# Folding later batches at the end of the first layer, with the shared tokens' unfolded queries in a stationary tile of their own

## The chip, the cores and the metric

One core of one Trainium2 chip runs the whole program. The metric is device time in microseconds (us), the median of several executions; lower is better. PE is TensorE (matmuls; PEld its weight loads), DVE is VectorE, ACT is ScalarE, POOL is GpSimd, SP issues most of the DMAs.

## The reference

Eight batches, eight heads, 576 tokens, 64 dimensions for each head, all in float32.

```python
q_s = softmax(q, over the 64 dimensions);  k_s = softmax(k, over the 576 tokens)
x   = q_s @ (k_s^T @ v)                      # per batch and head, then heads side by side: 576 x 512
u   = x + real(fft(fft(x, over tokens), over the 512 columns))
un  = (u - mean(u)) / sqrt(var(u) + 1e-6)    # over the 512 columns
out = u + relu(un @ w_ch1) @ w_ch2           # 512 -> 2048 -> 512
```

## The kernel before

**Tokens.** Of the 576 tokens of a batch, 512 lie in four "own" tiles of 128 rows, x(c, u) with c and u in 0 and 1. The other 64 are "shared" tokens: those of two batches fill one tile of 128 rows, and the four such tiles of all batches make a ninth group of the same size as a batch. The two layers run over groups in the order: batches 0 to 6, the shared group, batch 7.

**Attention** (`attention`, L430) is a list of steps for keys (four pairs of heads), shared queries (every other batch, for two batches at once) and own queries. The keys' softmax times v goes into `kvr`, a tile of four 128x128 blocks, one for a pair of heads. Own queries are exponentiated (L599), transposed on PE (L623), copied by ACT (L630), multiplied by `kvr` (L658) and copied by ACT to x (L665). For shared queries, `t_turn` (L633) transposes and copies both batches' 64 tokens into the columns 64 to 127 of `F`, and `t_fold` (L638) makes sums and differences of mirrored tokens, which the Fourier transform needs, into the columns 0 to 63 (17, 16, 16 and 15 of them, packed). So `F` holds, for each of four pairs of heads and each of two batches, one stationary tile of 128 columns: 64 folded, 64 unfolded. `t_times_kv` (L667), the last step of attention, multiplies them by `kvr` in four matmuls (L673): rows 0 to 63 of the result are the folded tokens, rows 64 to 127 are this batch's shared tokens. ACT copies the result to `g` (L676), and its lower half to the shared tile xs (L677). DVE then folds the columns of `g` (L678, L680, L681).

**Transform** (`transform`, L686). For batches after the first it is a list: four fold steps, one step that does nothing (batches 2 to 7), five blocks. The folds are `tokens_folded` (L699: sums on POOL, differences on DVE, of the own tiles), `columns_folded` (L705), `by_frequency` (L714) and `folded`, which makes the last DVE folds (L720, L721) and starts the next batch's first two key loads, each with a tiny DVE instruction (`gate`, L495) that ties the keys' use to the fold. The blocks are matmuls with the cosine and sine tables `ft` (L752 with the folded own tokens, L755 with `g`). Then follow the transform over columns (`mix_own`, `mix_shared`), which adds to x, and `norm` (statistics, normalization, transposes and the sums of its quarters, L369 to L372).

**Layers.** From the second group on, both layers (`up`, L945, and `down`, L982) use seven half-size products in place of eight (`strassen`, L906), in the order 1, 6, 5, 7, 2, 4, 3, over three PSUM banks `ba`, `bb` and `bc`. The first layer is four jobs of seven products, each product eight matmul instructions of 256 columns; the second layer is one job of seven products of 32 such instructions. (A float32 matmul in the code is two instructions in the profile.) Products 6, 7 and 4 add up in `bb`: after 6, DVE reads the bank into `u2` (L925), after 7 into `u3` (L929), and 7 and 4 are then added to the bank by matmuls without a start. In the first layer DVE adds the results (L968), ACT applies relu (L964, L969), and POOL makes the sums that the second layer's products need (`a_side`, L362 to L365). In the second layer POOL adds intermediate values to x (L1007).

**Order.** The main function (L1054) mixes lists: `one` is the attention of the next batch, `two` the transform, mixes and, behind them, `norm` of the next group. `merged(flat(jobs), one)` spreads `one` evenly over the first layer's steps, `merged(down, two + ...)` spreads the others over the second layer's. The program is then built by a framework that keeps each engine's queue in an order of its own planning, with priorities that follow this order, so that neighbouring steps may change places. Each engine then takes its queue in order. The first group (batch 0 in the layers, batch 1 in attention and transform) has hand-written gaps in place of `merged`.

Of the kernel before, what the change touches and what calls it, by code (L numbers as in the profile page):

```python
# [40 lines left out]
F32 = mybir.dt.float32  # L41
I32, U32 = mybir.dt.int32, mybir.dt.uint32
ACT = mybir.ActivationFunctionType
ALU = mybir.AluOpType
AX = mybir.AxisListType

P = 128
B, H, S, DH = 8, 8, 576, 64
D = H * DH
FF = 4 * D  # L50
NR = H // 2
# [5 lines left out]
MO = S // 4  # L57
ME = MO + 1
Q = 32
W = 2 * Q  # L60
NT = Q // 2 + 1
# [22 lines left out]
def mixed(main, side):  # L84

    steps = []
    for i, step in enumerate(main):
        steps.append(step)
        steps += side[i * len(side) // len(main):(i + 1) * len(side) // len(main)]
    return steps  # L90


def merged(main, side):
    for step in mixed(main, side):
        step()
# [28 lines left out]
class _Block:  # L124
    def __init__(self, ctx, tc, q, kT, v, w1, w2, ft, cd, out):
        self.nc, self.tc = tc.nc, tc
        self.q, self.kT, self.v, self.w1, self.w2, self.out = q, kT, v, w1, w2, out
        self.ft_dram, self.cd_dram = ft, cd
        nc = self.nc
        pool = lambda name, **kw: ctx.enter_context(tc.tile_pool(name=name, bufs=1, **kw))  # L130
        self.const, self.work, self.small = pool("const"), pool("work"), pool("small")
        self.ps = pool("ps", space=bass.MemoryType.PSUM)
        self.dram = pool("dram", space=bass.MemoryType.DRAM)
        c = self.const
        self.ident = c.tile([P, P], F32, name="ident")
        make_identity(nc, self.ident[:])
        self.eps = c.tile([P, 1], F32, name="eps")
        nc.gpsimd.memset(self.eps[:], LN_EPS)
        self.kvr = []
        for b in range(2):  # L140
            t = c.tile([P, NR, P], F32, name=f"kvr{b}")
            nc.gpsimd.memset(t[:], 0.0)
            self.kvr.append(t)

        self.sn = []
        for i in range(2):
            t = c.tile([P, NN], F32, name=f"sn{i}")
            nc.gpsimd.memset(t[:], 0.0)
            self.sn.append(t)

        self.ZT = c.tile([P, KT, P], F32, name="ZT")

        self.Zr, self.ZTr = c.tile([P, HD], F32, name="Zr"), c.tile([P, P], F32, name="ZTr")
        self.kss = [c.tile([P, NC, P], F32, name=f"ks{i}") for i in range(2)]
        for t in (self.Zr, self.ZTr):
            nc.gpsimd.memset(t[:], 0.0)
        for t in self.kss:
            nc.gpsimd.memset(t[0:64, 4, :], 0.0)

        self.T, self.F = c.tile([P, 2 * NR, 4, NT], F32, name="T"), c.tile([P, 2 * NR, P], F32, name="F")  # L160
        nc.gpsimd.memset(self.T[:], 0.0)

        self.sign = c.tile([P, 1], F32, name="sign")
        nc.gpsimd.memset(self.sign[:], -1.0)
        nc.gpsimd.memset(self.sign[0:Q + 1], 1.0)
        d = self.dram
        self.w1s = [d.tile([P, 7, HD], F32, tag=f"w1s{p}", name=f"w1s{p}", bufs=1) for p in range(NP)]
        self.w2s = d.tile([7, P, NP, HD], F32, tag="w2s", name="w2s", bufs=1)

        self.big = c.tile([P, 3 * NF * D], F32, name="big")  # L170
        part = lambda i: self.big[:, i * NF * D:(i + 1) * NF * D].rearrange("p (f n) -> p f n", n=D)
        self.w1sb, self.w2sb, self.h0 = part(0), part(1), part(2)
        self.ft = c.tile([P, 4 * NM], F32, name="ft")
        self.cd = c.tile([P, 5 * QD + 1], F32, name="cd")
        self.xs, self.live, self.stream = {}, {}, {}
        self.turns = 0
        self.unused = None

        self.later = []

        self.words = [self.work.tile([P, 2, D], F32, tag=n, name="words", bufs=k) for n, k in (("xs", 2), ("x", 4), ("x", 4))]
# [122 lines left out]
    def tables(self):  # L304
        self.nc.sync.dma_start(self.ft[:], self.ft_dram)
        self.nc.sync.dma_start(self.cd[:], self.cd_dram)
# [326 lines left out]
    def t_turn(self, it):  # L633
        pt = self.turned_q(it)
        self.live.pop(it)
        self.nc.scalar.copy(self.F[:, :, W:], pt[:].rearrange("p r (e t) -> p (r e) t", t=W))

    def t_fold(self, it):  # L638

        V, G, T, F = self.nc.vector, self.nc.gpsimd, self.T, self.F  # L640
        q = F[:, :, W:]
        V.tensor_copy(T[:, :, 0:2, 0], q[:, :, 0:Q + 1:Q])
        for e, op, i in ((G, ALU.add, 0), (V, ALU.subtract, 2)):
            e.tensor_tensor(out=T[:, :, i, 1:NT], in0=q[:, :, 1:NT], in1=q[:, :, W - 1:W - NT:-1], op=op)
            e.tensor_tensor(out=T[:, :, 1 + i, 1:NT - 1], in0=q[:, :, Q - 1:Q - NT + 1:-1],
                            in1=q[:, :, Q + 1:Q + NT - 1], op=op)
        n = NT - 1
        pair = lambda a, step: F[:, :, a:a + 2 * step].rearrange("p r (k t) -> p r k t", t=step)[:, :, :, 0:n]
        V.tensor_tensor(out=pair(NT, NT + n - 2), in0=T[:, :, 0:3:2, 0:n], in1=T[:, :, 1:4:2, 0:n], op=ALU.subtract)
        G.tensor_tensor(out=pair(1, Q), in0=T[:, :, 0:3:2, 1:NT], in1=T[:, :, 1:4:2, 1:NT], op=ALU.add)  # L650
        V.tensor_tensor(out=F[:, :, 0:1], in0=T[:, :, 0, 0:1], in1=T[:, :, 1, 0:1], op=ALU.add)

    def q_times_kv(self, it):
        nc, (_, b, c, u) = self.nc, it
# [12 lines left out]
    def t_times_kv(self, b):  # L667
        nc, V = self.nc, self.nc.vector
        j, kvr = b % 2, self.kvr[b % 2]
        part = slice(W * j, W * j + W)  # L670
        px = self.acc((P, D))
        for r in range(NR):
            nc.tensor.matmul(px[:, r * P:(r + 1) * P], lhsT=self.F[:, 2 * r + j], rhs=kvr[:, r, :], start=True,  # L673
                             stop=True)
        g = self.halves()
        nc.scalar.copy(g[:, 0:D], px)  # L676
        nc.scalar.copy(self.xshared(b // 2)[part], px[W:])  # L677
        V.scalar_tensor_tensor(out=g[:, 1:HD], in0=g[:, D - 1:HD:-1], scalar=self.sign[:, 0:1], in1=g[:, 1:HD],  # L678
                               op0=ALU.mult, op1=ALU.add)
        V.tensor_tensor(out=g[:, NN:NN + QD], in0=g[:, 0:QD], in1=g[:, HD:QD:-1], op=ALU.subtract)  # L680
        V.tensor_tensor(out=g[:, 0:QD], in0=g[:, 0:QD], in1=g[:, HD:QD:-1], op=ALU.add)  # L681
        self.live["g", b] = g
# [371 lines left out]
def kernel(ctx: ExitStack, tc: tile.TileContext, q, kT, v, w1, w2, ft,  # L1054
# [27 lines left out]
    def norm(g):  # L1082
        def make():
            nexts[g], steps = blk.norm(g)
            return steps
        return late(make, 7)

    def flat(steps):
        return [s for step in steps for s in step]
# [17 lines left out]
    one, two = front(0)  # L1107
# [5 lines left out]
    for order, g in enumerate(groups):  # L1113
        loads = [] if g == 0 else None
        one, two = front(order + 1, loads) if order + 1 < B else (blk.later, [])
        if g == 0:
# [6 lines left out]
            n = 2 * NF - 10  # L1123
# [6 lines left out]
            turn = (0, 16, 19, 21, 23, 25)  # L1130
# [13 lines left out]
            at = 0  # L1144
# [15 lines left out]

        jobs, down = blk.up(order, nexts.pop(g)), blk.down(g, order)

        merged(flat(jobs), one)
        merged(down, two + (norm(groups[order + 1]) if order < B else []))


def tables():

    turn = lambda a, b, n: 2.0 * np.pi * (np.outer(a, b) % n) / n
    odd = np.concatenate([np.arange(129, 160, 2), np.arange(1, 128, 2), np.arange(287, 160, -2)])  # L1170
    even = np.concatenate([[0], np.arange(130, 159, 2), [288], np.arange(2, 129, 2), np.arange(286, 159, -2)])
    ft = np.zeros((P, 4 * NM), np.float32)
    a = turn(1 + np.arange(P), np.concatenate([odd, even]), S)
    ft[:, :NM], ft[:, NM:2 * NM] = np.cos(a), np.sin(a)
    row = P + np.arange(NT)
    row[0] = n = 0

    for i, (f, m, at, rows) in enumerate(((np.cos, even, MO, row), (np.cos, odd, 0, row[:-1]), (np.sin, odd, 0, row[1:]),
                                          (np.sin, even, MO, row[1:-1]))):
        at += (2 + i // 2) * NM  # L1180
        ft[n:n + len(rows), at:at + len(m)] = f(turn(rows, m, S))
        n += len(rows)
    d, n = np.arange(P), np.arange(QD)
    cd = np.zeros((P, 5 * QD + 1), np.float32)
    cd[:, :QD] = np.cos(turn(d, 2 * n + 1, D))
    cd[:, QD:NN] = np.cos(turn(d, 2 * np.arange(QD + 1), D))
    cd[:QD - 1, NN:NN + QD - 1] = np.sin(turn(d[1:], 2 * n[1:], D))
    cd[:, NN + QD - 1:D] = np.sin(turn(d + 1, 2 * n + 1, D))
    cd[:, D:] = 1.0 - 2.0 * (np.arange(QD + 1) % 2)
    return ft, cd  # L1190
# [28 lines left out]
```

## Time and profile before

| what | value |
|---|---|
| median of 3 runs (lowest to highest) | 1128.05 us (1124.97 to 1131.2) |
| profiled execution, its own time | 1128.05 us |
| its span, first to last instruction | 1126.2 us |
| mean granted PE clock | 0.991 |
| DMA, mean over the span | 172 GB/s |
| one period (a group's two layers) in the middle, 322.6 to 442.7 us | 120.1 us |

The busy share of an engine is an average over the span; the table of stretches in the next section gives it for single stages. The head, about 88 us, is batch 0's attention, transform and norm, with the weights' loads under way; then come batch 0's two plain layers until 199 us; then eight groups of two layers with seven products each.

### The profile page before, as it was taken

To read this page: it belongs to the slowest core of one execution; us is meant where nothing else is said; L and a number is where in the kernel's file an instruction comes from. 1 tells how busy PE (TensorE), PEld (TensorE's weight loads), DVE (VectorE), ACT (ScalarE), POOL (GpSimd) and SP (SyncE) were. 2 spreads that over 40 slices of the span, in tenths; PEclk is the share of its full clock that TensorE was granted. 3 is DMA by queue.
4 is the path that set the end of the run, shared out by engine and by line. 5 is a ranking of instruction groups with operands and counts; after the bars stand their busy time and mean duration, and the time that the engine had idled before them with its cause. 6 is when DMAs were issued, how large, how long until landed. Compare 5 with 4: busy or idle time off the path is not lost.

```text
span 1126.2 us, 14461 instructions
## 1 busy us (share of the span) xinstructions
PE 1088.4 (97%) x5376; PEld 909.9 (81%) x5376; DVE 545.4 (48%) x1121; ACT 403.5 (36%) x973; POOL 331.9 (29%) x303
## 2 busy tenths in 40 slices
PE   5789989999999999999999999999999999999997
PEld 4644545887888888898889888888889888888886
DVE  6694796368423734375344643583444352103301
ACT  6695434255233513362325332542334152201200
POOL 1065571235013510324024402251034203402320
PEclk8899999999999999999999999999999999999999
DMA  9555786464246534554356435642453444434451
GB/s 305 176 190 188 259 291 220 145 224 166 98 150 211 195 127 145 195 172 171 125 173 221 150 106 190 198 185 108 147 191 150 144 144 144 187 141 157 152 187 56
DMA packets 92581, 193.79 MB, mean 172 GB/s; under 512 B 23120, under 2 KB 59728, under 8 KB 85344
## 3 DMA queue, kind: packets, MB, share of 16 engines
q1 hardware_dynamic: 90712, 191.82, 49.9%
q10 hardware_dynamic: 1800, 1.05, 0.3%
q8 instruction: 43, 0.70, 0.2%
q14 instruction: 26, 0.21, 0.1%
HBM read 168.72 MB, written 28.31 MB: 175 GB/s over the span
## 4 chain that ended last, share of the span: by engine, by line
PE 81%; POOL 3%; issue 2%; ACT 1%; DVE 1%; ACTq 0%; POOLq 0%
PE bb L957 14%; PE bb L995 14%; PE bc L995 10%; PE ba L957 9%; PE bc L957 9%; PE ba L995 9%; PE acc L568 2%; PE acc L658 2%; PE bc L896 2%; PE acc L752 1%; PE acc L776 1%; PE acc L755 1%; PE tr L857 1%; PE tr L554 1%; PE tr L623 1%
## 5 line engine op out<-in xcount | busy, mean ns | idle before, releaser
L957 PE MATMUL bb<-unT,big 128*128 128x256 f32 x768 | 187.4, 381 | 0.2 <-DVE u L925 0.2
L995 PE MATMUL bb<-big 128*128 128x256 f32 x768 | 172.1, 379 | 0.0
L957 PEld LDWEIGHTS bb<-unT,big 128*128 128x128 f32 x768 | 142.8, 190 | 23.9 <-DVE u L925 3.0
L995 PEld LDWEIGHTS bb<-big 128*128 128x128 f32 x768 | 145.4, 190 | 20.3
L362 POOL TENSOR_TENSOR big<-big 128x512 f32<-128x512 f32 (+1 forms) x38 | 46.2, 1216 | 307.6 <-ACT big L969 306.8
L969 ACT ACTIVATE big<-big 128x512 f32<-128x512 f32 x96 | 60.3, 629 | 182.7 <-DVE big L968 182.2
L957 PE MATMUL bc<-unT,big 128*128 128x256 f32 x512 | 125.4, 379 | 0.0
L957 PE MATMUL ba<-unT,big 128*128 128x256 f32 x512 | 123.6, 379 | 0.2 <-ACT unT L861 0.2
L995 PE MATMUL bc<-big 128*128 128x256 f32 x512 | 116.0, 379 | 0.5 <-DVE x L1012 0.5
L995 PE MATMUL ba<-big 128*128 128x256 f32 x512 | 114.8, 379 | 0.0
L929 DVE TENSOR_TENSOR u<-bb,s 128x512 f32<-128x512 f32 x40 | 27.6, 691 | 173.1 <-PE bb L995 116.1
L995 PEld LDWEIGHTS bc<-big 128*128 128x128 f32 x512 | 96.1, 190 | 14.3 <-DVE x L1012 0.9
L995 PEld LDWEIGHTS ba<-big 128*128 128x128 f32 x512 | 95.7, 190 | 12.1
L957 PEld LDWEIGHTS bc<-unT,big 128*128 128x128 f32 x512 | 95.1, 190 | 12.6
L957 PEld LDWEIGHTS ba<-unT,big 128*128 128x128 f32 x512 | 95.1, 190 | 12.2 <-ACT unT L861 0.5
L370 POOL TENSOR_TENSOR unT<-unT 128x512 f32<-128x512 f32 x8 | 14.2, 1772 | 179.8 <-DVE unT L369 179.8
L607 ACT ACTIVATE q<-q,qm 128x64 f32<-128x64 f32 x240 | 61.6, 338 | 6.8 <-DVE qm L605 6.6
L925 DVE TENSOR_TENSOR u<-bb,s 128x512 f32<-128x512 f32 x40 | 27.5, 688 | 71.7 <-PE bb L957 38.7
L968 DVE TENSOR_TENSOR big<-bc,u 128x512 f32<-128x512 f32 x64 | 44.1, 689 | 22.8 <-PE bc L957 21.7
L1007 POOL TENSOR_TENSOR x<-x,u 128x512 f32<-128x512 f32 x14 | 17.7, 1267 | 118.8 <-DVE u L929 99.0
L861 ACT COPY unT<-tr 128x512 f32<-128x512 f32 x36 | 20.7, 585 | 79.9 <-PE tr L857 79.3
L968 DVE TENSOR_TENSOR big<-bb,s 128x512 f32<-128x512 f32 x32 | 22.1, 691 | 56.1 <-PE bb L957 56.1
(254 smaller groups left out, 1640.8 us busy)
## 6 DMA issues: line engine op xcount, KB each, us to landing
big<-w1s SPq DMA_DIRECT2D x64, 896.0 KB
big<-w2s SPq DMA_DIRECT2D x56, 1024.0 KB
big<-in_w_dram SPq DMA_DIRECT2D x21, 512.0 KB
q<-in_q_dram SPq DMA_DIRECT2D x27, 256.0 KB
k<-in_kT_dram SPq DMA_DIRECT2D x24, 288.0 KB
v<-in_v_dram SPq DMA_DIRECT2D x24, 256.0 KB
words<-in_w_dram SPq DMA_DIRECT2D x8, 512.0 KB
mirror<-x SPq DMA_DIRECT2D x14, 256.0 KB
```

Source lines behind the costliest of these rows:

```text
L362: e1.tensor_tensor(out=to(4), in0=at(2), in1=at(3), op=ALU.add)
L568: nc.tensor.matmul(pk, lhsT=ks[:, c, :], rhs=v[:, c, :], start=(c == 0), stop=(c == NC - 1))
L607: nc.scalar.activation(heads[:, h, :], heads[:, h, :], ACT.Exp, bias=m[:, h:h + 1])
L658: nc.tensor.matmul(px[:, r * P:(r + 1) * P], lhsT=qT[:, r, :], rhs=self.kvr[b % 2][:, r, :], start=True, stop=True)
L861: nc.scalar.copy(unT[:, u:u + 3:2, :, cols], pt[:].rearrange("p (a k) t -> p a k t", a=2))
L896: nc.tensor.matmul(po[:], lhsT=h[:, f, i * P:(i + 1) * P], rhs=self.w2sb[:, f, :], start=(f == 0), stop=(f == NF - 1))
L925: V.tensor_tensor(out=temp("u2"), in0=box["bb"][:], in1=box["s1"][:], op=ALU.add)
L929: V.tensor_tensor(out=temp("u3"), in0=box["bb"][:], in1=box["s1"][:], op=ALU.add)
L957: nc.tensor.matmul(bank()[:, i, :], lhsT=w[:, WA_AT[m], k * P:(k + 1) * P], rhs=unT[:, B_AT[m], k, :], start=first and i == 0 and k == 0, ...
L968: V.tensor_tensor(out=hp(i), in0=bank[:], in1=u[:], op=ALU.add)
L969: nc.scalar.activation(hp(i), hp(i), ACT.Relu)
L995: nc.tensor.matmul(bank()[:, i, :], lhsT=h[p][:, A_AT[m], i * P:(i + 1) * P], rhs=w[:, p, :], start=first and i == 0 and p == 0, stop=p == ...
```

## The change

`F` is laid out anew: for each pair of heads and batch, four blocks of 32 columns, 17 of them used, and nothing unfolded; it is zeroed at the start. The unfolded transposed queries of both batches go to a new tile `tq`, from which `t_fold` reads. `t_times_kv` multiplies `F` by `kvr` in four matmuls as before, and then, in a new group of four into another PSUM buffer, `tq` by `kvr`; ACT copies the 64 rows that belong to this batch to xs. The last fold instructions of `t_fold` are one on each of POOL and DVE in place of one on POOL and two on DVE. Signs and tables follow the new layout. In the main loop, for the groups after the first, the first four steps of `two`, the folds, are put behind attention in `one`, so that they are spread over the end of the first layer and not over the start of the second; this concerns batches 2 to 7.

```diff
-        self.T, self.F = c.tile([P, 2 * NR, 4, NT], F32, name="T"), c.tile([P, 2 * NR, P], F32, name="F")
-        nc.gpsimd.memset(self.T[:], 0.0)
+        self.T, self.F = c.tile([P, 2 * NR, 4, NT], F32, name="T"), c.tile([P, 2 * NR, 4, Q], F32, name="F")
+        for t in (self.T, self.F):
+            nc.gpsimd.memset(t[:], 0.0)
...
-        nc.gpsimd.memset(self.sign[:], -1.0)
-        nc.gpsimd.memset(self.sign[0:Q + 1], 1.0)
+        nc.gpsimd.memset(self.sign[0:W], 1.0)
+        nc.gpsimd.memset(self.sign[W:], -1.0)
...
     def t_turn(self, it):
         pt = self.turned_q(it)
         self.live.pop(it)
-        self.nc.scalar.copy(self.F[:, :, W:], pt[:].rearrange("p r (e t) -> p (r e) t", t=W))
+        self.tq = self.work.tile([P, NR, P], F32, tag="tq", name="tq", bufs=1)
+        self.nc.scalar.copy(self.tq[:], pt[:])
 
     def t_fold(self, it):
 
         V, G, T, F = self.nc.vector, self.nc.gpsimd, self.T, self.F
-        q = F[:, :, W:]
-        V.tensor_copy(T[:, :, 0:2, 0], q[:, :, 0:Q + 1:Q])
-        for e, op, i in ((G, ALU.add, 0), (V, ALU.subtract, 2)):
+        q = self.tq[:].rearrange("p r (e t) -> p (r e) t", t=W)
+        V.tensor_copy(T[:, :, 0:3:2, 0], q[:, :, 0:Q + 1:Q])
+        for e, op, i in ((G, ALU.add, 0), (V, ALU.subtract, 1)):
             e.tensor_tensor(out=T[:, :, i, 1:NT], in0=q[:, :, 1:NT], in1=q[:, :, W - 1:W - NT:-1], op=op)
-            e.tensor_tensor(out=T[:, :, 1 + i, 1:NT - 1], in0=q[:, :, Q - 1:Q - NT + 1:-1],
+            e.tensor_tensor(out=T[:, :, 2 + i, 1:NT - 1], in0=q[:, :, Q - 1:Q - NT + 1:-1],
                             in1=q[:, :, Q + 1:Q + NT - 1], op=op)
-        n = NT - 1
-        pair = lambda a, step: F[:, :, a:a + 2 * step].rearrange("p r (k t) -> p r k t", t=step)[:, :, :, 0:n]
-        V.tensor_tensor(out=pair(NT, NT + n - 2), in0=T[:, :, 0:3:2, 0:n], in1=T[:, :, 1:4:2, 0:n], op=ALU.subtract)
-        G.tensor_tensor(out=pair(1, Q), in0=T[:, :, 0:3:2, 1:NT], in1=T[:, :, 1:4:2, 1:NT], op=ALU.add)
-        V.tensor_tensor(out=F[:, :, 0:1], in0=T[:, :, 0, 0:1], in1=T[:, :, 1, 0:1], op=ALU.add)
+        for e, op, i in ((G, ALU.add, 0), (V, ALU.subtract, 1)):
+            e.tensor_tensor(out=F[:, :, i::2, 0:NT], in0=T[:, :, 0:2], in1=T[:, :, 2:4], op=op)
...
         g = self.halves()
         nc.scalar.copy(g[:, 0:D], px)
-        nc.scalar.copy(self.xshared(b // 2)[part], px[W:])
+        px = self.acc((P, D))
+        for r in range(NR):
+            nc.tensor.matmul(px[:, r * P:(r + 1) * P], lhsT=self.tq[:, r, :], rhs=kvr[:, r, :], start=True, stop=True)
+        nc.scalar.copy(self.xshared(b // 2)[part], px[part])
...
         jobs, down = blk.up(order, nexts.pop(g)), blk.down(g, order)
 
+        if order + 1 < B:
+            one, two = one + two[:4], two[4:]
         merged(flat(jobs), one)
         merged(down, two + (norm(groups[order + 1]) if order < B else []))
```

The rest of the diff puts the rows of the table `ft` where the new layout has its columns; the table's size stays.

## The prediction

> **What bounds the kernel now.** I read the page's busy shares and slices first, then busy time by stage, then the timeline of one hand-over from first to second layer.
>
> ```profile
> PE 1088.4 (97%) x5376; PEld 909.9 (81%) x5376; DVE 545.4 (48%) x1121; ACT 403.5 (36%) x973; POOL 331.9 (29%) x303
> PE   5789989999999999999999999999999999999997
> ...
> 322.60:384.30 61.70, 61.70 (x342) 54.94 (x341) 29.33 (x57) 27.16 (x68) 20.86 (x17) 1.00 0.57 182
> 384.30:442.70 58.40, 58.40 (x302) 51.86 (x301) 26.86 (x66) 15.53 (x39) 11.40 (x9) 1.00 0.42 148
> 973.60:1022.00 48.40, 48.40 (x229) 42.60 (x229) 7.18 (x9) 3.35 (x6) 10.60 (x8) 1.00 0.47 169
> ```
>
> The columns of the last three are stretch, length, then busy us of PE, weight loads, DVE, ACT, POOL. From 199 us on PE runs without gaps at clock 1.00. Nothing removed from another engine can shorten a stretch where PE never waits; whatever is put on PE, or makes it wait, is added in full. Idle PE is 22 us before 88 us, 5 us from there to 199, 6 us in the tail.
>
> The timeline of the same kernel where batch 3's attention ends and its fold begins (start us, us, engine, line):
>
> ```profile
> 383.05 1.08 PEld L673 LDWEIGHTS acc<-kvr,F 128*128 128x128 f32 x8
> 383.26 1.05 PE L673 MATMUL acc<-kvr,F 128*128 128x128 f32 x8
> 384.15 7.07 PE L995 MATMUL ba<-big 128*128 128x256 f32 x32
> 384.46 0.57 ACT L676 COPY eo<-acc 128x512 f32<-128x512 f32 x1
> 385.64 0.48 DVE L678 SCALAR_TENSOR_TENSOR eo<-eo,sign 128x255 f32<-128x255 f32 x1
> 385.88 1.37 POOL L362 TENSOR_TENSOR big<-big 128x512 f32<-128x512 f32 x1 [2.34 <-ACT big L969]
> 386.04 1.76 DVE L699 TENSOR_TENSOR eo<-x 128x512 f32<-128x512 f32 x1
> 391.41 2.36 DVE L705 TENSOR_TENSOR eo<-eo 128x255 f32<-128x255 f32 x2
> 393.69 0.28 DVE L720 TENSOR_TENSOR eo<-eo 128x128 f32<-128x128 f32 x1
> 394.76 0.48 DVE L720 TENSOR_TENSOR eo<-eo 128x128 f32<-128x128 f32 x2
> ```
>
> The eight L673 matmuls hold PE 0.89 us (383.26 to 384.15), so 0.111 us each; L957's eight of 256 columns take 1.73 us. The DVE fold takes 9.3 us (385.64 to about 394.95), beside a product of 32 matmuls (6.9 us) and more. PE does not notice.
>
> Batch 4's hand-over, where POOL is the later one:
>
> ```profile
> 507.64 1.27 POOL L362 TENSOR_TENSOR big<-big 128x512 f32<-128x512 f32 x1 [9.80 <-ACT big L969]
> 516.62 1.66 POOL L714 TENSOR_TENSOR eo<-eo 128x257 f32<-128x257 f32 x2
> 518.48 0.68 DVE L720 TENSOR_TENSOR eo<-eo 128x128 f32<-128x128 f32 x3
> ```
>
> And in the first layer, DVE's u2 (L925) between products:
>
> ```profile
> 370.68 1.89 PE L957 MATMUL bb<-unT,big 128*128 128x256 f32 x8
> 372.66 0.69 DVE L925 TENSOR_TENSOR u<-bb,s 128x512 f32<-128x512 f32 x1 [3.44 <-PE bb L957]
> 373.73 1.89 PE L957 MATMUL bc<-unT,big 128*128 128x256 f32 x8
> 375.46 1.89 PE L957 MATMUL bb<-unT,big 128*128 128x256 f32 x8
> ```
>
> The seventh product at 375.46 adds to the bank that u2 has just read (L933 to L937), so it may not start before u2 ends. Today DVE is idle 3.44 us ahead of u2, which ends at 373.35, 2.1 us early. Between bb's first and second product lies only one product, 1.73 us in this layer; in the second layer it is 6.9 us.
>
> **What the skill says.** "SBUF — State Buffer", section "SBUF: two separate sides", says that VectorE instructions with two SBUF inputs and GpSimd instructions take one shared port pair by an exclusive lock, the loser blocking entirely. The trace agrees: L699 on DVE takes 0.69 us at 34.61 us, with POOL idle, and 1.76 us at 386.04, with POOL in L362. "Perfetto Trace Analysis", section "Identifying the Most-Contended Engine", says that matmul busy share does not measure how full PE is, and weight-load share does. The trace has 42.60 of 48.40 us (88%) in a stage with nothing but products: PE is the limit. "TensorE: Matmul & The Clock Gate", section "Back-to-back issue gap", says that spacing is set by load and matmul together; its 81 ns for 128 columns is not what float32 shows here, 111 ns, which I use.
>
> **The change, part by part.** The sum stands against the profiled run's own time, 1128.05 us, which is also the median; its span is 1126.2 and 1.85 us lie around it. Which instruction stands before which I take from the built programs.
>
> 1. Four more matmuls for each of eight batches, 8 instructions of 0.111 us: 0.89 us. Six batches run where PE has no gap (5.3 us); batch 1's lies in the first group's second layer, almost full (0.9); batch 0's at 26 us among gaps, from 0 to 0.9, I take 0.4. Together 6.6 us. The ACT copy to xs (0.58) is as before. F's memset of 1024 columns is about twice T's 0.55 us, at 3.4 us on a POOL idle until 19.44: nothing. L651 goes from DVE (0.43 us, four times), and L649/L650 keep their size: nothing, PE is the limit.
>
> 2. The fold of batches 3, 5 and 7. In the built program DVE has it ahead of u2 of the first layer's last job. Count from t = 0, the end of that job's predecessor. PE: L673 0.89, the new group 0.89, then three products of 1.73: the seventh product is wanted at 6.97. DVE: L676 on ACT follows L673, so L678 starts at 1.75; POOL is then full with a_side and its own folds (four of 1.3, the rest of two L705, two L714 of 0.9), as it was from 385.88 to 393.49, so I take the same 9.3 us up to u2: u2 from 11.05 to 11.75, PE goes on at 11.95. Stall 5.0 us. Then u3 (L929) stands behind five short L720/L721 (1.0), two gates (0.25), L609 (0.67), two L542 (1.35), in 3 and 5: it ends 4.0 after u2, PE wants it after two products, 3.66: 0.4 more. 5.4 + 5.4 + 5.0 = 15.8. Without port conflicts the same instructions (two L699 at 0.69, four L705/L714 at 0.41, L678 at 0.48, five at 0.28, overlapping by some 0.07) take 4.2 us and the stall is nothing; with conflicts as in batch 2 (L678 1.49, L680 1.24 us) it is 7.5. The keys' loads and gates move with the fold, but SP has the loads ahead of the second layer's weights in both programs (L514 at 360.39, L420 at 366.95): nothing. Waiting on SP's late q loads (DVE waited 8.0 us in 8 of these) may add up to 1.5 a batch; cover is the wait for L676, so I take nothing.
>
> 3. Batches 4 and 6: L673 stands inside the last job's first product. From L673's end PE wants the seventh product after 0.89 + 0.86 + 1.73 + 1.73 = 5.2. The L720 just ahead of u2 needs POOL's first L714, behind L362 to L365, two L699 and two L705. These start at 0.25 (after L969) and take 10.8, as from 507.64 to about 517.5 with one L699 more: L720 ends at 11.4, u2 at 12.1, PE goes on at 12.3. Stall 7.1, and 0.9 for u3, behind 3.5 us of L714, L720, L721 and L609: 8.0 each, 16.0. Undisturbed POOL gives 5.8 each, conflicts 10.
>
> 4. Batch 2: its fold stays at the second layer's start, but the transform (L752) now follows one product, not two. L752 is wanted 0.89 + 6.9 = 7.8 us after L673. Before, the fold ended 15 us after it (278.94 against 263.9), of which 1.3 was waiting for POOL, which now folds earlier. I take 12.5: stall 4.7, less the 1.4 which PE waits there today: 3.3. Ends: -1.4 and 6.
>
> 5. The second layer's start has an emptier DVE; PE never waits there except in batch 2, so no gain. Denser attention in the first layer may cost up to 0.8 a batch (PE waits 0.6 on L555 in batch 4 today); I take nothing.
>
> Sum: 6.6 + 15.8 + 16.0 + 3.3 = 41.7. 1128.05 + 41.7 = 1169.8 us.
>
> **The rivals.** A: port conflicts fade, since POOL gets through its part earlier. Then batches 3, 5, 7 stall not at all, 4 and 6 by 5.8, batch 2 gains 1.4: 6.6 + 11.6 - 1.4 = 16.8, 1144.9 us. For it: DVE's uncontended 0.69. Against: POOL has the same work beside it before. B, not slower: the fold is done before u2 is due, in every batch. The point is 5.2 us from L678's start to u2's end in batch 3. Then only matmuls count, less batch 2's 1.8 us of idle PE: 6.6 - 1.8 = 4.8, 1132.9 us, within the bound. Against: POOL's chain alone takes 10 us in batch 4. C: the delay goes on, through q loads, attention and u3: 7.5 x 3 + 10 x 2 + 6 + 6.6 + 9 = 64, 1192 us.
>
> **How the numbers follow.** The forecast (1152 to 1182 by itself) has 0.72, A 0.13, C 0.10, B 0.05. About 0.5% (5.6 us) is what a measurement of this kernel can tell from no change. B's chance is 0.04 for no change and 0.01 for a gain. The range goes from A's value to short of C's: 1145 to 1188.
>
> **What would show it.** In the changed profile: PE waiting for DVE L925's counterpart once in each of batches 3 to 7, by 5 to 7 us, more in 4 and 6; smaller waits for L929's; a wait of L752 in batch 2 of 3 to 6 us; 64 more PE matmul records of 128 columns, PE busy up by 7 us, PE busy below the stretch in first-layer stages alone; L699 on DVE near 1.7 us. If PE waits nowhere for u2, or DVE's fold takes under 5 us, the prediction is wrong.

## The result, and the profile after

The changed kernel takes 1189.72 us (median of 4 runs, 1187.94 to 1190.33), beside 1128.6 us for the kernel before on the same chip (4 runs): ratio 1.054, interval 1.051 to 1.057. The profiled execution has 1189.83 us, a span of 1188.0 and a mean clock of 0.979. The forecast was 1169.8 in a range of 1145 to 1188: right in direction and place, some 20 us too small. In this kernel's listing L927 is what was L925 (u2), L754 was L752, L678 is the new group, L680, L682 and L683 fold the columns of `g`; the other lines moved by one or two. "Batch 3's first layer" is, here and below, the first layer beside which batch 3's attention runs; the data in the layer itself are batch 2's.

The page: PE's busy time, and its granted clock in 40 slices.

```profile
PE 1108.6 (93%) x5440; PEld 923.7 (78%) x5440; DVE 532.8 (45%) x1117; ACT 405.4 (34%) x973; POOL 335.3 (28%) x304
PEclk9999999898999899989999999989999999999999
```

Busy time by stage (stretch, length, then busy us of PE, weight loads, DVE, ACT, POOL, then the clock): batch 3's first layer and the second layer behind it.

```profile
335.17:405.17 70.00, 65.03 (x349) 57.09 (x348) 39.43 (x81) 29.11 (x70) 23.32 (x19) 0.95 0.49 160
405.17:463.52 58.35, 58.35 (x301) 51.81 (x300) 16.76 (x42) 14.30 (x37) 9.41 (x8) 1.00 0.42 150
```

Before, PE was busy for 61.70 of 61.70 us in the first of these. Now it stands still for 5.0 us, and its clock is 0.95. The second layer lost 10 us of DVE work and is as long as before, 58.35 us: its engine was PE already. All the loss lies in the first layers, and in both layers of batch 2.

What PE waited for (engine, what for, us in total, times, longest):

```profile
PE bb L959 <- DVE u L927: 31.1, 5, 7.8
PE tr L555 <- ACT k L545: 5.4, 8, 2.3
PE acc L754 <- DVE eo L723: 4.8, 1, 4.8
```

The five waits for u2 are 4.8, 7.8, 4.8, 7.5 and 6.3 us in batches 3 to 7; forecast were 5.0, 7.1, 5.0, 7.1, 5.0. Batch 3's hand-over, by the timeline:

```profile
388.29 1.21 DVE L701 TENSOR_TENSOR eo<-x 128x512 f32<-128x512 f32 x1
388.92 1.72 POOL L364 TENSOR_TENSOR big<-big 128x512 f32<-128x512 f32 x1
389.43 1.35 DVE L683 TENSOR_TENSOR eo<-eo 128x128 f32<-128x128 f32 x1
392.73 1.44 POOL L366 TENSOR_TENSOR big<-big 128x512 f32<-128x512 f32 x1
392.97 1.35 DVE L722 TENSOR_TENSOR eo<-eo 128x128 f32<-128x128 f32 x1
395.12 0.28 DVE L722 TENSOR_TENSOR eo<-eo 128x128 f32<-128x128 f32 x1
395.32 0.68 DVE L927 TENSOR_TENSOR u<-bb,s 128x512 f32<-128x512 f32 x1
396.05 3.78 PE L959 MATMUL bb<-unT,big 128*128 128x256 f32 x8 [4.76 <-DVE u L927]
```

Two things are to be read here. The same L722 takes 1.35 us at 392.97, while POOL is in the last of its four sums (L366), and 0.28 us at 395.12, when POOL is done. And PE's eight matmuls behind the wait span 3.78 us, not 1.89. The stretches that follow, with PE's clock third from the end, tell why:

```profile
396.00:398.00 2.00, 1.95 (x5) 1.58 (x6) 2.00 (x9) 0.00 (x0) 0.00 (x0) 0.50 0.02 4
398.00:400.00 2.00, 2.00 (x6) 1.58 (x5) 1.18 (x3) 1.57 (x4) 0.00 (x0) 0.50 0.00 0
400.00:402.00 2.00, 2.00 (x10) 1.73 (x9) 2.00 (x9) 0.13 (x2) 0.00 (x0) 0.91 0.00 0
```

PE is busy and advances at half rate: the granted clock is 0.50. Over batches 2 to 7, in slices of 0.5 us, PE's still time is 45.1 us (4.1 before), and its busy time times the missing share of the clock adds up to 16.1 us (0 before).

### The profile page after: what moved, and what is told of

The parts are those of the page before. It is cut to its first block, busy times and chain, and to the rows that moved or that the text cites. A ratio compares the mean times of both kernels' runs of the same rounds, so it can differ in the third digit from the quotient of the medians.

```text
span 1188.0 us, 14574 instructions
## 1 busy us (share of the span) xinstructions
PE 1108.6 (93%) x5440; PEld 923.7 (78%) x5440; DVE 532.8 (45%) x1117; ACT 405.4 (34%) x973; POOL 335.3 (28%) x304
## 4 chain that ended last, share of the span: by engine, by line
PE 77%; DVE 7%; POOL 3%; issue 3%; ACT 2%; DMA 1%; SPq 0%; ACTq 0%; POOLq 0%; DVEq 0%
PE bb L997 14%; PE bb L959 13%; PE bc L997 9%; PE ba L997 9%; PE ba L959 8%; PE bc L959 8%; PE acc L569 2%; PE bc L898 2%; PE acc L657 2%; PE acc L754 2%; PE acc L757 1%; PE acc L778 1%; PE tr L859 1%; PE tr L555 1%; PE tr L624 1%
## 5 line engine op out<-in xcount | busy, mean ns | idle before, releaser
L959 PE MATMUL bb<-unT,big 128*128 128x256 f32 x768 | 195.7, 394 | 31.1 <-DVE u L927 31.1
L959 PEld LDWEIGHTS bb<-unT,big 128*128 128x128 f32 x768 | 149.4, 198 | 55.1 <-DVE u L927 34.2
L997 PE MATMUL bb<-big 128*128 128x256 f32 x768 | 176.0, 382 | 0.0
L959 PE MATMUL ba<-unT,big 128*128 128x256 f32 x512 | 126.1, 384 | 0.2 <-ACT unT L863 0.2
L959 PE MATMUL bc<-unT,big 128*128 128x256 f32 x512 | 125.4, 379 | 0.0
L959 PEld LDWEIGHTS ba<-unT,big 128*128 128x128 f32 x512 | 97.5, 194 | 13.4 <-ACT unT L863 0.5
L959 PEld LDWEIGHTS bc<-unT,big 128*128 128x128 f32 x512 | 95.1, 190 | 11.8
L927 DVE TENSOR_TENSOR u<-bb,s 128x512 f32<-128x512 f32 x40 | 27.6, 690 | 149.5 <-PE bb L997 98.0
L931 DVE TENSOR_TENSOR u<-bb,s 128x512 f32<-128x512 f32 x40 | 27.6, 690 | 89.8 <-PE bb L959 63.7
L371 POOL TENSOR_TENSOR unT<-unT 128x512 f32<-128x512 f32 x8 | 14.2, 1775 | 155.7 <-DVE unT L370 155.7
L923 ACT COPY s<-ba 128x512 f32<-128x512 f32 x40 | 23.4, 584 | 100.5 <-PE ba L959 62.8
L970 DVE TENSOR_TENSOR big<-bc,u 128x512 f32<-128x512 f32 x64 | 44.1, 689 | 26.7 <-PE bc L959 25.9
```

The lines of the kernel that those rows point to most:

```text
L927: V.tensor_tensor(out=temp("u2"), in0=box["bb"][:], in1=box["s1"][:], op=ALU.add)
L931: V.tensor_tensor(out=temp("u3"), in0=box["bb"][:], in1=box["s1"][:], op=ALU.add)
L959: nc.tensor.matmul(bank()[:, i, :], lhsT=w[:, WA_AT[m], k * P:(k + 1) * P], rhs=unT[:, B_AT[m], k, :], start=first and i == 0 and k == 0, ...
L970: V.tensor_tensor(out=hp(i), in0=bank[:], in1=u[:], op=ALU.add)
L997: nc.tensor.matmul(bank()[:, i, :], lhsT=h[p][:, A_AT[m], i * P:(i + 1) * P], rhs=w[:, p, :], start=first and i == 0 and p == 0, stop=p == ...
```

## The experiments

The theory after the result: the move costs nearly everything, by three terms. u2 stands behind a fold on DVE that POOL slows, PE runs at half rate (granted clock 0.50) after each wait, and batch 2 has losses of its own. Rivals: the new layout is the cause; the half rate is no loss of its own; DVE's own queue, and not POOL, makes the fold long; the fold costs its time anywhere near the border.

**The move alone and the layout alone.** In the kernel before, only this was added:

```diff
         jobs, down = blk.up(order, nexts.pop(g)), blk.down(g, order)
+        if order + 1 < B:
+            one, two = one + two[:4], two[4:]
```

> The kernel before with one edit: four steps of each later batch's fold go to the end of the first layer; the shared tokens' queries stay in one stationary tile. Theory (the move costs nearly all, in three parts: about 31 us of waits for u2, some 2 to 3 us of half-rate matmuls behind each of them, and a longer first layer in batch 2): 1186 us, within 1180 to 1190, with the waits of the second layer's first products on u2 of 4 to 8 us in each of batches 3 to 7 and a granted clock near 0.95 in those first layers. Rival (the new layout, with its second group of matmuls and other fold operations, costs the larger part): under 1145 us.

Measured: 1175.75 us, ratio 1.043 (1.040 to 1.046). The second kernel is the changed one without these two lines.

> The changed kernel without the move: the layout of the queries and the second group of 128-column matmuls alone. Theory: the matmuls add 7 x 0.9 = 6.3 us and the head gives back about 2.8 us as it did in the changed kernel, so 1132 us, within 1129 to 1136, and no new waits for u2. Rival (the layout is the cause): above 1150 us.

Measured: 1129.05 us, ratio 1.0021 (1.0011 to 1.0032), no new waits. So the layout isn't the cause, and its 6 us of matmuls are not even all seen: its batch 2 stands still for 0.6 us where the kernel before does for 2.9. But the move alone costs 49 us where I expected 60: the two don't add up. The reason is the order that the framework plans. In batch 4, the move alone has u2 fifth on DVE after the first instruction of the fold, ahead of the L705 pair. DVE rows of that kernel:

```profile
518.28 0.68 DVE L925 TENSOR_TENSOR u<-bb,s 128x512 f32<-128x512 f32 x1
518.88 1.75 DVE L705 TENSOR_TENSOR eo<-eo 128x255 f32<-128x255 f32 x2
```

The changed kernel has it eighth, behind that pair (L707 there) and an L722 that waits for POOL:

```profile
528.59 0.29 DVE L722 TENSOR_TENSOR eo<-eo 128x128 f32<-128x128 f32 x1 [2.10 <-POOL eo L716]
528.80 0.68 DVE L927 TENSOR_TENSOR u<-bb,s 128x512 f32<-128x512 f32 x1
```

PE's wait there is 3.7 us in the one and 7.8 in the other, and the waits for u2 add up to 21.8 us in place of 31.1. Why the framework plans so is not shown. Batch 2, too, loses less in this profile: its first layer keeps clock 1.00. That part need not come from the edit. In the profile of the run with the filled wait below, where all engines have the changed kernel's instructions in the changed kernel's order until that wait, batch 2's 2.34 us wait is not followed by half rate either; it comes 26 us later, behind the wait of 2.15 us, and costs 1.7 us there in place of 3.2.

**Batch 2 alone.**

```diff
-        if order + 1 < B:
+        if order == 1:
             one, two = one + two[:4], two[4:]
```

> The changed kernel with the move for batch 2 alone, whose attention is the only one with K and V of a batch to build beside it; batches 3 to 7 keep their fold beside the second layer. Theory (batch 2 has a loss of its own, 9 us in its first layer and 6 in its second): 1146 us, within 1141 to 1150. Rival (batch 2 loses nothing by the move, its stages are longer by the matmuls and the border alone): 1132 to 1135 us.

Measured: 1146.45 us, ratio 1.0169 (1.0133 to 1.0204). Against the layout alone, batch 2's move costs 17.4 us, of which the two stages show 10.3 as additional still time and 6.1 as half rate. The attention is spread over fewer of the first layer's steps than before, since the fold's four stand behind it. In the three runs below that spread it as before, batch 2's first layer stands still for 0.6 us, not 6.1. Why batch 2 loses so much more by it than the others is not shown. PE rows of the changed kernel:

```profile
226.26 1.12 PE L555 MATMUL tr<-ident,k 128*128 128x128 f32 x4 [2.34 <-ACT k L545]
228.11 2.50 PE L569 MATMUL acc<-v,ks 128*128 128x128 f32 x10 [0.52 <-ACT ks L556]
230.40 1.91 PE L959 MATMUL ba<-unT,big 128*128 128x256 f32 x4
```

The keys' exponential on ACT (L545) needs the maximum from DVE (L543), which stands behind DVE's L970 and so behind the product that has just ended; PE has the transposes (L555) next in its queue and waits. The half rate follows here too: four matmuls (L959) span 1.91 us, not 1.03.

**The half rate by itself.** In batch 7, 14 matmuls whose result nothing reads fill the wait ahead of the last job's seventh product:

```diff
+            if j == 3 and at == 6:
+                job[3].insert(0, lambda: self.warm(self.ft[:, 0:256], 14))
```

> The changed kernel with 14 additional matmuls of 128 by 256, whose result nothing reads, ahead of the last product of batch 7's first layer's border, where TensorE waits for u2; batch 7 alone. Theory (behind the wait TensorE runs at half rate for some 3.4 us, since it stood still): the filled wait keeps the granted clock at 1.00, and batch 7's first layer shortens from 71.8 us to 69.2 to 69.6, though it does more work. Rival (the wait alone is the loss, the half rate is no loss of its own): unchanged or longer, 71.8 us or more.

Measured: batch 7's first layer 69.42 us (71.84 in the changed kernel; the first layers of batches 3 to 6, where nothing was edited, differ by 0.4 us at most between these two profiles), and 1186.65 us in all (ratio 1.0537, 1.051 to 1.0564; the single edit is not to be told from the changed kernel by that). By stretches, the changed kernel where the wait ends (917.63 us), then this kernel where it ends (913.09):

```profile
916.00:919.00 3.00, 1.37 (x3) 1.18 (x4) 2.97 (x10) 0.00 (x0) 0.49 (x1) 0.50 0.01 3
919.00:922.00 3.00, 3.00 (x8) 2.36 (x7) 0.67 (x2) 0.00 (x0) 0.00 (x0) 0.50 0.00 0
909.00:912.00 3.00, 3.00 (x15) 2.64 (x14) 2.97 (x4) 0.00 (x0) 2.87 (x4) 1.00 0.00 0
912.00:915.00 3.00, 2.77 (x13) 2.10 (x13) 2.54 (x10) 0.00 (x0) 0.00 (x0) 1.00 0.01 3
```

u2 came no earlier: PE's useful work paused for 6.4 us (906.65 to 913.09), as it did for 6.3 in the changed kernel. Only the clock differs, 1.00 in place of 0.50 for the 5 us that follow the pause, and 2.4 us are gained by doing more. The half rate is a loss of its own.

**What makes the fold long.** First, the changed kernel without one quarter of POOL's sums in the first layers of batches 3 to 7 (so some of the second layer's operands are not computed):

```diff
-            def other(i, hp=hp):
+            def other(i, hp=hp, j=j):
...
-                    if i == 2:
+                    if i == 2 and not (j == 2 and 2 <= at <= 6):
                         self.a_side(hp, hp, nc.gpsimd, nc.gpsimd)
```

> The changed kernel, which leaves out, in the first layers of batches 3 to 7, one of the additions of a folded operand that run beside the fold (the third job's), so a part of the second layer's operands is not computed. Theory (VectorE's fold is slowed by GpSimd's operations beside it, and in batches 4 and 6 waits for them): the waits for u2 shrink, by 3 us or more in batches 4 and 6 and by up to 4 in 3, 5 and 7. Rival (VectorE's own queue sets u2): waits unchanged at 4.8 to 7.8 us.

Measured: 1157.1 us, ratio 1.0279 (1.0259 to 1.0299); waits for u2 4.8 us in all, in place of 31.1. DVE rows of this kernel in batch 3:

```profile
388.68 0.68 DVE L701 TENSOR_TENSOR eo<-x 128x512 f32<-128x512 f32 x1
389.28 0.28 DVE L683 TENSOR_TENSOR eo<-eo 128x128 f32<-128x128 f32 x1
390.15 0.28 DVE L722 TENSOR_TENSOR eo<-eo 128x128 f32<-128x128 f32 x1
391.43 0.68 DVE L927 TENSOR_TENSOR u<-bb,s 128x512 f32<-128x512 f32 x1
```

The same twelve instructions stand ahead of u2 as in the changed kernel, in the same order, and take 5.2 us from the first one's start (386.26) to u2, in place of 9.45 (385.87 to 395.32). L683 and the first L722 take 0.28 us in place of 1.35 each, the second L701 0.68 in place of 1.21. DVE's own work would nearly have fitted: PE's wait there is 0.5 us, not 4.8.

Then the same sums, all computed, but on DVE:

```diff
-            def other(i, hp=hp):
+            def other(i, hp=hp, j=j):
...
                     if i == 2:
-                        self.a_side(hp, hp, nc.gpsimd, nc.gpsimd)
+                        e = V if j == 2 and 2 <= at <= 6 else nc.gpsimd
+                        self.a_side(hp, hp, e, e)
```

> The changed kernel, whose four additions of the third job's folded operand in the first layers of batches 3 to 7 are done on VectorE, where they stand in the fold's queue, in place of GpSimd; all is computed. Theory (the fold is long because GpSimd's additions slow VectorE's, 1.35 in place of 0.28 us and 1.75 in place of 0.68): VectorE gets 4 x 0.68 = 2.7 us more to do in that queue and u2 still comes earlier; waits for u2 of 3 us or less in batches 4 and 6 (7.8 before), 3.5 or less in the others; 1155 to 1172 us. Rival (the work in VectorE's own queue sets u2): each wait grows by up to 2.7 us, above 1195 us.

Measured: 1156.79 us, ratio 1.0279 (1.0264 to 1.0295); waits for u2 7.6 us in all, the longest 2.4. DVE takes 0.68 us for a sum where it has no POOL beside it (1.21 where it has), POOL took 1.3 to 1.8. Doing the sums on DVE saves some 30 us (ratio 1.0279 to the kernel before, in place of 1.0541), as much as leaving them out. In this run the planned order changed too (u2 now comes ahead of a part of the fold), and in batches 4 and 6 of both runs POOL's own chain, which the fold waited for, became shorter. So the slowed DVE is shown for batch 3; in 4 and 6 it can't be parted from the shorter chain.

**The fold anywhere near the border.** The four steps in one go behind the first layer; the attention is spread as before:

```diff
-        if order + 1 < B:
-            one, two = one + two[:4], two[4:]
         merged(flat(jobs), one)
+        if order + 1 < B:
+            for step in two[:4]:
+                step()
+            two = two[4:]
```

> The changed kernel with one edit: the four moved steps are issued in one go after the first layer's last step, so that VectorE has u2 and u3 of the second layer's first products ahead of them, and the attention is spread over the whole first layer as in the kernel before. Theory (the order on VectorE is the cause: u2 stands behind the fold): 1132 to 1140 us, no wait for u2 over 1 us in batches 3 to 7, and a granted clock of 1.00 there. Rival (any place near the border of the layers costs the same, since the fold then holds up u2's successors): above 1150 us.

Measured: 1171.94 us, ratio 1.0395 (1.0363 to 1.0427). u2 was no longer waited for, as my theory had it, and the time was the rival's. PE's wait had moved to the fold's next reader:

```profile
PE acc L754 <- DVE eo L723: 31.0, 6, 6.5
```

With four steps less, the second layer's list brings the first transform matmul behind its first 32 matmuls, 7 us after the border; in batch 3 the fold's last instruction ends 11 us after it (402.4 against 391.3), and in batch 2, whose attention reaches 3.2 us into the second layer, the fold is done 16 us after it (276.9 against 260.5). I tried to move that reader with one empty step (`two = [lambda: None] + two[4:]`):

> The changed kernel with the four moved steps issued in one go after the first layer's last step, as in the run before that had them there, and one empty step ahead of the second layer's share of the attention, so that the first matmul that reads the fold comes some 13 us after the border of the layers in place of 7. Theory (a fold in one go costs only as far as its first reader, u2's product or the attention's matmul, stands less than the fold's 10 to 13 us behind it): no wait for the fold over 2 us and no half rate in batches 2 to 7, 1129 to 1136 us. Rival (a fold in one go delays VectorE's other work at the border, whoever reads it): above 1145 us.

Measured: 1168.48 us, ratio 1.0389 (1.0369 to 1.0409), with 30.9 us of waits: the edit had no effect, since the planned order still had L754 behind 32 matmuls. It decides nothing. With four empty steps it stands behind 64:

> As the run with the four steps in one go after the first layer, with four empty steps (one had not moved the attention's first matmul) ahead of the second layer's share of the attention, which puts its first matmul behind 64 of the second layer's in place of 32, that is some 14 us after the border, where it stood without the move. Theory (a fold in one go costs only where its first reader stands less than the fold's 10 to 13 us behind it): waits for the fold of 1 us or less, granted clock 1.00, 1128 to 1135 us. Rival (a fold in one go at the border holds up more than its readers): above 1145 us.

Measured: 1128.48 us, ratio 1.0015 (1.0001 to 1.0029), as the layout alone. No wait for the fold is left, and the clock is 1.00 in batches 2 to 7. The PE rows of batch 3's border in this kernel:

```profile
382.37 7.07 PE L997 MATMUL ba<-big 128*128 128x256 f32 x32
389.28 7.07 PE L997 MATMUL bb<-big 128*128 128x256 f32 x32
396.18 0.66 PE L754 MATMUL acc<-ft,eo 128*128 128x144 f32 x4
```

DVE's last fold instruction runs at 393.21, 3 us before L754. The fold is as crowded and as slow as in the run with 1171.94 us: in batch 3 each of its DVE instructions takes the same time in both, to 0.02 us. The four empty steps also put off what stands behind the transform in the list, but PE's waits name the fold alone: 7 us more between it and its first reader are worth 43 us, of which the run with 1171.94 us shows 31.0 as waits for the fold and 10.3 as half rate.

**Two tries for a faster kernel.** The kernel before has clock 0.73 to 0.78 between 20 and 40 us, the changed one 1.00, and batch 0's plain layers ended 2.8 us earlier in it. So the kernel before, with

```diff
+        self.warm(self.kvr[0][:, 0:2, :], 18)
         last = self.t_rows(b, tail, nc.scalar)
```

> The kernel before with 18 additional matmuls at the start of its first products, whose result nothing reads, so that TensorE does not stand still there. Theory (the kernel before loses 2.8 us in its head because the granted clock was 0.76 between 20 and 40 us, and the changed one does not): 1 to 3 us faster than before. Rival (the head's end is set by transfers and the clock there is a symptom): no change within 1 us, or slower by the added matmuls.

Measured: 1133.2 us, ratio 1.0067 (1.005 to 1.0083): slower. PE still waited there, 9.3 us for one transpose, and batch 0's layers ended at 203.4 us, not 198.7. The rival holds. The kernel before with the fold of the 1128.48 us run:

> The kernel before, in its own layout, with the four steps in one go after the first layer and four empty steps ahead of the second layer's share of the attention. Theory: the matmuls of the second group are gone (7 x 0.9 = 6.3 us less than the same with the new layout, whose head was 3 us shorter than the kernel before's), and the kernel before's 2.9 us of standing still in batch 2 shrink to 0.6 as they did there; 1122 to 1126 us, 0.2 to 0.4% faster than before if the head doesn't differ. Rival (the matmuls bound both alike, the waits in batch 2 come back elsewhere): within 1 us of before, or slower by new waits.

Measured: 1125.42 us, ratio 0.9999 (0.999 to 1.0009): the rival again. Batch 2 stands still for 2.9 us as in the kernel before; that belongs to the old layout, not to the fold's place. Batch 0's layers ended at 194.5 us here, at 195.0 with the move alone and at 198.7 in the profile of before, all three in the same layout, and between 195.1 and 198.7 in the profiles with the new one: this part differs between executions, and the changed kernel's 2.8 us are no work of the change.

## Why the prediction was wrong in size

1. *Four more matmuls for each batch, 6.6 us*: right where it was measured. Each instruction has 0.11 us (L678's eight hold PE 0.89 us from 385.05 to 385.94), and the layout alone lengthens batch 3's first layer by 0.90 us.
2. *Batches 3, 5 and 7, 15.8 us*: u2's waits were 15.8 (15.0 forecast), u3's nothing (0.8). The working held for batches 3 and 5, DVE's 9.3 us of fold up to u2 included (9.45 in batch 3); batch 7's wait was 1.3 us longer than forecast, and I did not follow it. That the fold's total came out is in part luck: in batch 3 L701 takes 0.68 and 1.21 us, not near 1.7, and the first L722 takes 1.35 where it took 0.28 before. u3 is hidden because PE needs more time for the two products ahead of it, at half rate, than I had; in batch 3 DVE waits 0.82 us for PE ahead of it (L931 at 399.87).
3. *Batches 4 and 6, 16.0 us*: u2 15.3 (14.2 forecast), u3 nothing (1.8). POOL's chain set it, as forecast; the run with the move alone shows that the planned order counts beside it.
4. *Batch 2's L752, net 3.3 us*: 4.8 less 1.4, 3.4.
5. *The failed steps.* In the first part I wrote that what makes PE wait "is added in full", and in step 2 that "PE goes on" when u2 is there: at the full rate, by the sum. It goes on at half, and that term, 16.1 us, was missing. The prediction's own sign shows it: PE's busy time was to rise by 7 us, and rose by 20.2. The filled wait in batch 7 shows that it is real (2.4 us in one place), and the trace's clock shows it behind seven waits: u2's five, L752's in batch 2, and the 2.34 us in batch 2's attention. "TensorE: Matmul & The Clock Gate", section "What's actually happening", says that PE's clock falls to half after an idle window of about 3.4 us and rises after a busy one; the trace agrees on the size (periods of half rate of 3.4 or 6.8 us, where the forecast waits were 4.7 and more). The sum should have priced it for each wait.
6. *Step 5, denser attention: "I take nothing"*: batch 2's first layer stands still for 6.1 us (1.5 before), and 4 and 6 for 0.6 us each beyond u2 and what they did before. 5.9 us in all. I had bounded it at 0.8 a batch from batch 4, whose keys are not in batch 2's position, and didn't follow batch 2's keys through DVE's queue. The runs that spread the attention as before have none of it.

From the kernel before's 1126.2 us of span, the table sums the changed kernel's:

| term | forecast | measured |
|---|---|---|
| new matmuls (from 199 us on, six batches; forecast: all) | 6.6 | 5.3 |
| waits for u2 | 29.2 | 31.1 |
| waits for u3 | 2.6 | 0 |
| L752 in batch 2, net | 3.3 | 3.4 |
| other still time, batch 2's attention above all | 0 | 6.5 |
| half rate behind the waits | 0 | 16.1 |
| ahead of 199 us, and the tail | 0 | -3.0 |
| rest, 0.3 to 0.5 us for each batch | 0 | 2.4 |
| sum | 41.7 | 61.8 |

Other still time is what u2 and L752 leave of the 41.0 us of additional still time in batches 2 to 7. The last row is only what is left over, and stays unexplained.

Rival A (conflicts fade) gets its answer from the two runs with a quieter POOL: there the fold nearly fits in batch 3, with 0.5 and 0.9 us of wait, but in the changed kernel POOL is not quiet. Rival B's condition, the fold done before its reader, came true in the run with four empty steps, and there the time was B's sort (1128.48). Rival C had the size nearly right (1192) by luck: no delay went on through q loads or u3.

## What to carry to other kernels

Work that is moved on a side engine is priced by the distance from its end to its first reader on the bounding engine, in both places: the same fold cost 43 us or nothing with its reader 7 or 14 us after the border. When TensorE is made to wait for more than some 4 us, add the matmuls that then run at half rate, 1.6 to 2.9 us for each such wait in the changed kernel; shorter waits may cost it or not. And where VectorE's time is critical, look at what GpSimd does beside it: four sums for each of five batches, 2.7 us each time on a VectorE without company, cost the kernel some 30 us on GpSimd.

## What the runs showed of the hardware beside that

- The half rate doesn't follow a wait's length alone. In the eight traces of kernels that lost time by the move, it came behind all 26 waits of PE of 4.5 us or more between 199 us and the tail, behind 4 of the 6 of 3.4 to 3.8 us, and behind 6 of the 13 of 2.1 to 2.4 us. In the run with the fold in one go, PE waited 3.45 us for L754 in batch 3 and then ran at half rate for 3.4 us; it waited 3.46 us in batch 5 and kept the full rate. "TensorE: Matmul & The Clock Gate", section "What's actually happening", has a window that runs free; the two waits agree with that. Waits of 2.1 to 2.4 us are less than the 3.4 us of the page's idle window, and were at times enough.
- Two-input DVE instructions beside POOL: 1.35 us against 0.28 for 128x128, 1.21 to 1.75 against 0.68 for 128x512, by the same line in the same run. The shorter one loses most in proportion. In batch 3, L683 and L722 end 0.14 and 0.15 us after the sum on POOL beside them (L364 at 390.64, L366 at 394.17). That agrees with the exclusive lock of "SBUF — State Buffer", section "SBUF: two separate sides": an instruction then waits for the end of one of POOL's, which take 1.3 to 1.8 us here, however short it is itself.
